# Two parts of the rows side by side in every other block of first products, experts of 208 and 192 slots

## The chip, the cores and the metric

The kernel runs on one core of a Trainium2 chip. TensorE (PE, with its weight loads as PEld) multiplies, VectorE (DVE) and ScalarE (ACT) read its sums out of PSUM, GpSimd (POOL) works on SBUF and issues indirect DMAs, SyncE (SP) issues most other DMAs. The metric is the device time of one execution in microseconds (us); lower is better.

## What is computed

A linear-attention recurrence, then two mixture-of-experts layers of 8 experts (1536 rows of 384, hidden width 1024). The change concerns the first of the layers alone:

```python
h = np.maximum(np.einsum('ecd,edf->ecf', disp, w1), 0.0)
y = np.einsum('ecf,efd->ecd', h, w2)
```

The first line is what is called "first products" here, the second "second products".

## The kernel before, in words

**Jobs.** The 16 experts (8 of layer 1, 8 of layer 2) are jobs 0 to 15, one after the other on TensorE. Jobs 0 and 1 have 240 slots; jobs 2 to 7 take the other six experts in order of their number of rows and have 240, 224, 208, 208, 192 and 192 slots (`CAPS`). So jobs 4 and 5 have 208 columns, 6 and 7 have 192. In the profiled execution job 4 starts at 159.5 us, job 5 at 176.7, job 6 at 194.4, job 7 at 211.0 and job 8 at 227.6.

**Split numbers.** TensorE multiplies fp32r numbers, which are rounded. To keep fp32 precision, each weight and each row is split into a high part (rounded, a copy by ScalarE, L537 for weights and L635 for rows) and a low part (the rest, a subtraction by GpSimd or VectorE, L538 and L636). A product is then high x high + low weight x high row + high weight x low row.

**First products (`hidden`).** A job has 8 blocks of 128 hidden columns, f = 0 to 7. A block is 9 matmuls into one PSUM bank: three parts of the depth (d), each with three products (six at L683, then the three with the low rows at L686). ScalarE then writes the rectified sum's high part (L692, "relu" below) and VectorE its low part (L693, "subtract"); both read the bank. There are three such banks (`ph`), used in turn: block f + 3 can start when VectorE's subtract of block f has ended.

**Second products (`second`).** For each f, three output parts: one matmul with the high weights over both halves of the hidden block side by side (2c columns, L714), one with the low weights over its high half (c columns, L716). In PSUM the two halves of the result stay apart; `job_route2` adds them when it reads them out (L841 on ScalarE, L842 on VectorE).

**What lies between.** Each engine takes its instructions strictly in the order in which the code issues them. Between the blocks of job n stand the steps of the routing of job n - 1 (`route2`, a generator, stepped by the table `STEPS`): 6 fp32 matmuls that show as 12 rows at L750 after block 1, two scaled copies on ScalarE (L752), then a chain of some thirty small VectorE instructions, a few ScalarE ones (L766, L767, L773, L800), three small matmuls that count places (L813 to L817, on TensorE's queue behind the second products of f = 0 to 2), and four indirect DMAs from GpSimd that scatter the rows for layer 2. The L813 matmul needs `accs`, written by VectorE at L796. Also between the blocks stand the splits of the next job's weights (L537, L538), one for each block.

In TensorE's order a layer-1 job is: blocks 0 and 1, L750, blocks 2 to 7, second products of f = 0 to 2, L813 to L817, second products of f = 3 to 7.

Of the kernel before, what the change touches and what calls it, by code (L numbers as in the profile page):

```python
# [7 lines left out]
F32R = mybir.dt.float32r  # L8
# [3 lines left out]
AF = mybir.ActivationFunctionType  # L12
ALU = mybir.AluOpType
# [8 lines left out]
C1, T1 = 240, 2  # L22
# [12 lines left out]
NF, ND = F // 128, DM // 128  # L35
# [19 lines left out]
LR = (5, 6, 7, 5, 7, 8)  # L55
LX = 9
SP = 7
WG = 8
STEPS = ("0111122111110000", "1232210200000000", "0100000111100000", "0111000000000000")
ENGS = ("GGGGGGGGGGGVVVVG", "GGGGGGGGGGGGGGGG")  # L60
# [7 lines left out]
def body(tc, ap, cap, dbg=False, stop=False):  # L68
    nc = tc.nc
    V, A, G, PE = nc.vector, nc.scalar, nc.gpsimd, nc.tensor  # L70
    with ExitStack() as ctx:
# [15 lines left out]
        def hb(shape, dt=F32):  # L87
            return sb(shape, "h", 18, dt)

        def xb(shape, dt=F32):  # L90
            return sb(shape, "x", 4, dt)
# [8 lines left out]
        def ph():  # L100
            return ps("ph", 3)
# [355 lines left out]
        jobs = [(1, e) for e in range(E)] + [(2, e) for e in range(E)]  # L457
# [87 lines left out]
        def w1_of(n, f, d):  # L545
            hi, lo = parts[n, f // 4]
            c = (f % 4) * 128
            return hi[:, d, c:c + 128], lo[:, d, c:c + 128]
# [6 lines left out]
        xg, xsp, xr_ = {}, {}, {}  # L555
# [34 lines left out]
        def load_rows(eng, g, rows_, c, cols):  # L590
# [5 lines left out]
                eng.dma_start(g[:c - k * p, k:, cols], rows_(k * p, c)[:, None, cols])  # L596
            eng.dma_start(g[:, :k, cols], rows_(0, k * p).rearrange("(t p) d -> p t d", p=p)[:, :, cols])

        def load_x(n, eng):
            layer, e = jobs[n]  # L600
            nt_, p, c = dims(n)
            store = (xs1, xs2)[layer - 1]
            if not turned(n):
                g = sb([p, nt_, RW], "b6", 5)
                load_rows(eng, g, lambda a, b: store[e * R + a:e * R + b], c, slice(None))
            else:
                nb = -(-c // 32)
                rows_of = lambda eng, r: store[e * R:e * R + r] if place(n) is None else store[bass.ds(expert(n, eng) * R, r), :]
                w = RW if layer == 1 else RW - DM
                t6 = sb([128, nb * ND * 32 + nt_ * w], "b6", 5)  # L610
                g = t6[:p, nb * ND * 32:].rearrange("p (t d) -> p t d", t=nt_)
                if layer == 2:
                    g = few_of(g)
                load_rows(eng, g, lambda a, b: rows_of(eng.engine, nt_ * p)[a:b], c if layer == 1 else nb * 32,
                          slice(DM, None))
                x = xr_[n] = t6[:, :nb * ND * 32].rearrange("p (t d) -> p t d", t=nb)
                rows_ = rows_of(mybir.EngineType.SP, nb * 32)
                for b in range(4):
                    nc.sync.dma_start(x[b * 32:b * 32 + 32], rows_.rearrange("(t j) d -> j t d", j=32)[
                        :, :, b * ND * 32:(b + 1) * ND * 32])  # L620
            xg[n] = g
            xsp[n] = (xb([128, ND, c], F32R), xb([128, ND, c], F32R))

        def split_x(n, d):
            layer, e = jobs[n]
            nt_, p, c = dims(n)
            g, (xh, xl) = xg[n], xsp[n]
            ds = (d,)
            if turned(n):
                x = xr_[n][:, :, d * 32:d * 32 + 32]  # L630
                y = pm()[:, :x.shape[1] * 32]
                V.transpose(y.rearrange("p (t j) -> p t j", j=32), x)  # L632

                def high():
                    A.activation(xh[:, d, :], y[:, :c], AF.Copy)  # L635
                    rest.append(lambda: V.tensor_tensor(xl[:, d, :], y[:, :c], xh[:, d, :].bitcast(F32), op=ALU.subtract))  # L636

                rest.append(high)
                return
            xp = pm()  # L640
            for k, d in enumerate(ds):
                for t, sl, r in tiles(n):
                    PE.transpose(xp[:, k * c + sl.start:k * c + sl.stop], g[:r, t, d * 128:(d + 1) * 128],
                                 ident[:r, :r])
            m = lambda x: x[:, ds[0]:ds[-1] + 1, :].rearrange("p d c -> p (d c)")
            w = len(ds) * c
            A.activation(m(xh), xp[:, :w], AF.Copy)
            V.tensor_tensor(m(xl), xp[:, :w], m(xh).bitcast(F32), op=ALU.subtract)

        def first_x():  # L650

            at = [py()[:, :C1] for _ in range(ND)]
            for d in range(ND):
                for t in range(T1):
                    PE.matmul(at[d][:, t * P1:(t + 1) * P1], early[0][:, t, d * 128:(d + 1) * 128], ident[:P1, :P1],
                              start=(t == 0), stop=False, skip_group_check=True)
            yield
            n = N // 128
            for j in range(EARLY, n):
                for d in range(ND):  # L660
                    for i in range(2):
                        PE.matmul(at[d], late[j][:, i * DM + d * 128:i * DM + (d + 1) * 128], late[j][:, 2 * DM:],
                                  start=False, stop=(i == 1 and j == n - 1), skip_group_check=True)
                yield
            xg[0] = sb([P1, T1, RW], "b6", 5)
            nc.sync.dma_start(xg[0][:, :, DM:], xs1[:C1, DM:].rearrange("(t p) d -> p t d", p=P1))
            xh, xl = xsp[0] = (xb([128, ND, C1], F32R), xb([128, ND, C1], F32R))
            for d in range(ND):
                A.activation(xh[:, d, :], at[d], AF.Copy)
                V.tensor_tensor(xl[:, d, :], at[d], xh[:, d, :].bitcast(F32), op=ALU.subtract)  # L670
            yield
# [2 lines left out]

        def hidden(n, f):
            c = dims(n)[2]
            xh, xl = xsp[n]
            p = ph()[:, :c]
            k = 0
            for d in range(ND):  # L680
                wh, wl = w1_of(n, f, d)
                for (w, x) in ((wh, xh), (wl, xh)):
                    PE.matmul(p, w, x[:, d, :], start=(k == 0), stop=False)  # L683
                    k += 1
            for d in range(ND):
                PE.matmul(p, w1_of(n, f, d)[0], xl[:, d, :], start=False, stop=(d == ND - 1))  # L686
            if jobs[n][0] == 1:
                both = hb([128, 2 * c], F32R)
                hh, hl = both[:, :c], both[:, c:]
            else:  # L690
                both, hh, hl = None, hb([128, c], F32R), hb([128, c], F32R)
            A.activation(hh, p, AF.Relu)  # L692
            V.scalar_tensor_tensor(hl, p, 0.0, hh.bitcast(F32), op0=ALU.max, op1=ALU.subtract)  # L693
            hs[f] = (hh, hl, both)
# [531 lines left out]
        for n, (layer, e) in enumerate(jobs):  # L1226
# [37 lines left out]
            if n < 2 * E - 1:  # L1264
                for f in range(NF):
# [14 lines left out]
                    if n == E and f == 0:  # L1280
                        for _ in prev:
                            pass
                        it, fin, d = late_tokens(n, gl), None, 0
# [31 lines left out]
            else:  # L1315
                nt_, p, c = dims(n)
# [229 lines left out]
```

## Time and profile before

| | |
|---|---|
| median of 3 runs | 457.77 us (457.44 to 458.2) |
| the profiled execution | 457.52 us |
| its span, first to last instruction | 455.8 us |
| outside the span | 1.7 us |
| TensorE busy | 444.1 us, 97% of the span |
| VectorE, ScalarE, GpSimd busy | 275.5, 265.6 and 345.9 us |

The profiled execution is 0.25 us below the median of the runs. Matmuls overlap, so their rows are longer than the distance from one start to the next; that distance is what a matmul costs on TensorE.

### The profile page before, as it was taken

Reading aid. Unit: us, or ns where it says so; the run is one execution under the profiler, and the core shown is the slowest. Engines: PE = TensorE matmul, PEld = TensorE weight load, DVE = VectorE, ACT = ScalarE, POOL = GpSimd, SP = SyncE. Lnnn points to the kernel's source line nnn. Section 1 sums busy time; section 2 is a strip of 40 time slices with the busy share of each in tenths; the row PEclk is TensorE's granted clock in tenths of the full one; section 3 lists DMA queues with packets and bytes.
Section 4 is the critical chain, followed back from the end, with each engine's and each line's share of the span. In section 5 each row is a group of like instructions: output and inputs, shape, how many; then the busy total and the mean of one; then the engine's idle time right before and its main releaser. Section 6 shows DMA issues by size and latency. Waiting matters only on the chain.

```text
span 455.8 us, 9510 instructions
## 1 busy us (share of the span) xinstructions
PE 444.1 (97%) x3167; PEld 417.8 (92%) x3170; DVE 275.5 (60%) x909; ACT 265.6 (58%) x703; POOL 345.9 (76%) x433
## 2 busy tenths in 40 slices
PE   8999999999999999999999999999999999999992
PEld 4588888899999999999999999999999999999992
DVE  8999988666967867878866454343434343243350
ACT  4577788367776775786651468255454464664310
POOL 4435698585998989899943379989969699699932
PEclk9999999999999999999999999999999999999998
DMA  8975962769999977976421997649378393894143
GB/s 279 408 265 160 350 239 97 246 206 317 332 294 317 276 257 220 261 228 195 127 70 55 267 318 220 137 111 295 75 227 188 91 313 75 253 282 54 18 53 43
DMA packets 73587, 93.66 MB, mean 205 GB/s; under 512 B 31963, under 2 KB 56611, under 8 KB 73527
## 3 DMA queue, kind: packets, MB, share of 16 engines
q1 hardware_dynamic: 66854, 79.98, 57.1%
q0 software_dynamic: 6672, 12.97, 12.7%
q8 instruction: 27, 0.44, 0.4%
q14 instruction: 34, 0.27, 0.2%
HBM read 70.30 MB, written 20.02 MB: 198 GB/s over the span
## 4 chain that ended last, share of the span: by engine, by line
PE 95%; DVE 2%; ACT 1%; issue 1%; POOL 0%; POOLq 0%; ACTq 0%
PE ph L683 24%; PE py L722 22%; PE ph L686 12%; PE py L714 9%; PE py L716 4%; PE ph L170 4%; PE ph L309 3%; PE pm L750 3%; PE pm L385 2%; PE py L336 2%; PE py L362 2%; PE py L356 2%; PE py L303 1%; PE ph L1002 1%; PE ph L975 1%; PE py L334 1%
## 5 line engine op out<-in xcount | busy, mean ns | idle before, releaser
L538 POOL TENSOR_TENSOR s<-s,s 128x384 fp32r<-128x384 f32 x208 | 217.7, 1173 | 17.9 <-ACT s L537 16.5
L683 PE MATMUL ph<-x,s 128*128 128x240 f32 (+9 forms) x768 | 133.0, 308 | 0.3 <-DVE h L693 0.3
L537 ACT ACTIVATE s<-s 128x384 fp32r<-128x384 f32 x256 | 124.7, 516 | 9.2 <-DMA s<-w 5.5
L683 PEld LDWEIGHTS ph<-x,s 128*128 128x128 f32 x768 | 116.2, 189 | 1.8 <-DVE h L693 0.5
L693 DVE SCALAR_TENSOR_TENSOR h<-ph,h 128x240 fp32r<-128x240 f32 (+9 forms) x128 | 60.2, 470 | 81.7 <-ACT h L692 76.4
L692 ACT ACTIVATE h<-ph 128x240 fp32r<-128x240 f32 (+9 forms) x128 | 54.1, 423 | 72.0 <-PE ph L686 68.4
L686 PE MATMUL ph<-x,s 128*128 128x240 f32 (+9 forms) x384 | 76.2, 306 | 0.0
L158 POOL DMA_INDIRECT out<-b,m_ix x28 | 44.0, 1571 | 30.2 <-ACT b L878 8.7
L722 PE MATMUL py<-h,s 128*128 128x304 f32 (+4 forms) x360 | 65.4, 339 | 0.0
L722 PEld LDWEIGHTS py<-h,s 128*128 128x128 f32 x360 | 63.2, 188 | 0.8
L714 PE MATMUL py<-h,s 128*128 128x480 f32 (+3 forms) x192 | 61.5, 376 | 0.0
L686 PEld LDWEIGHTS ph<-x,s 128*128 128x128 f32 x384 | 60.9, 189 | 0.2
L716 PE MATMUL py<-h,s 128*128 128x240 f32 (+3 forms) x192 | 50.5, 263 | 0.0
L158 POOL DMA_INDIRECT xs<-b,m_si x32 | 32.3, 1010 | 17.0 <-DVE pm L832 10.5
L318 POOL TENSOR_SCALAR_AFFINE_SELECT h<-h 128x512 f32<-128x512 f32 x24 | 23.8, 1014 | 27.9 <-ACT h L317 27.9
L722 PE MATMUL py<-s,h 128*128 128x384 f32 x216 | 38.6, 338 | 0.0
L714 PEld LDWEIGHTS py<-h,s 128*128 128x128 f32 x192 | 36.1, 188 | 2.6
L636 DVE TENSOR_TENSOR x<-pm,x 128x384 fp32r<-128x384 f32 (+8 forms) x42 | 19.9, 473 | 29.8 <-ACT x L635 29.6
L722 PEld LDWEIGHTS py<-s,h 128*128 128x128 f32 x216 | 37.8, 188 | 0.0
L716 PEld LDWEIGHTS py<-h,s 128*128 128x128 f32 x192 | 36.6, 191 | 0.0
L538 DVE TENSOR_TENSOR s<-s,s 128x384 fp32r<-128x384 f32 x48 | 34.0, 729 | 0.8 <-ACT s L537 0.5
L635 ACT ACTIVATE x<-pm 128x384 fp32r<-128x384 f32 (+8 forms) x42 | 17.7, 420 | 23.6 <-DVE pm L632 20.3
(263 smaller groups left out, 604.0 us busy)
## 6 DMA issues: line engine op xcount, KB each, us to landing
s<-w SPq DMA_DIRECT2D x28, 768.0 KB
s<-w_2b SPq DMA_DIRECT2D x22, 768.0 KB
s<-w_1b SPq DMA_DIRECT2D x14, 768.0 KB
xs<-s SPq DMA_DIRECT2D x2, 1576.0 KB
out<-s SPq DMA_DIRECT2D x4, 768.0 KB
b<-xs SPq DMA_DIRECT2D x12, 156.0 KB
b<-xs SPq DMA_DIRECT2D x12, 144.0 KB
b<-b SPq DMA_DIRECT2D x44, 36.0 KB
```

Of the source, the lines that this page charges most:

```text
L158: st = G.indirect_dma_start(out=dst, out_offset=bass.IndirectOffsetOnAxis(ap=ix, axis=0), in_=src, in_offset=None, **kw)
L318: G.affine_select(a_, a_, pattern=[[0, 4], [1, 128]], compare_op=ALU.is_ge, fill=0.0, base=0, channel_multiplier=-1)
L537: A.activation(hi[sl], t[sl], AF.Copy)
L538: rest.append(lambda: (eng or V).tensor_tensor(lo[sl], t[sl], hi[sl].bitcast(F32), op=ALU.subtract))
L636: rest.append(lambda: V.tensor_tensor(xl[:, d, :], y[:, :c], xh[:, d, :].bitcast(F32), op=ALU.subtract))
L683: PE.matmul(p, w, x[:, d, :], start=(k == 0), stop=False)
L686: PE.matmul(p, w1_of(n, f, d)[0], xl[:, d, :], start=False, stop=(d == ND - 1))
L692: A.activation(hh, p, AF.Relu)
L693: V.scalar_tensor_tensor(hl, p, 0.0, hh.bitcast(F32), op0=ALU.max, op1=ALU.subtract)
L714: PE.matmul(yp[o][:, :2 * c], wh[:, sl], both, start=(f == 0), stop=(f == NF - 1), skip_group_check=True)
L716: PE.matmul(yp[o][:, :c], wl[:, sl], hh, start=False, stop=(f == NF - 1), skip_group_check=True)
L722: PE.matmul(out_, l, r, start=(f == 0 and k == 0), stop=(f == NF - 1 and k == 2))
```

## The change

In jobs 4 to 7 the odd blocks (f = 1, 3, 5, 7) of the first products are built as the second products already are: for each d one matmul with the high weights over the high and the low rows side by side (2c columns, 416 or 384) and one with the low weights over the high rows (c columns). That is 6 matmuls in place of 9. The bank then holds two halves, c columns that are nearly the sum and c columns of high weight x low row. ScalarE copies the second half to SBUF, VectorE adds it to the first half in PSUM, and then relu and subtract follow as before. Even blocks and all other jobs stay as they are. For layer 1 the high and low rows of a job now lie in one tile.

```diff
+SIDE = 208
...
+        def two_parts(layer, c):
+            if layer == 2:
+                return xb([128, ND, c], F32R), xb([128, ND, c], F32R)
+            x = xb([128, ND, 2, c], F32R)
+            return x[:, :, 0, :], x[:, :, 1, :], x
...
-            xsp[n] = (xb([128, ND, c], F32R), xb([128, ND, c], F32R))
+            xsp[n] = two_parts(layer, c)
...
         def hidden(n, f):
             c = dims(n)[2]
-            xh, xl = xsp[n]
-            p = ph()[:, :c]
+            xh, xl = xsp[n][:2]
+            bank = ph()
+            p = bank[:, :c]
             k = 0
-            for d in range(ND):
-                wh, wl = w1_of(n, f, d)
-                for (w, x) in ((wh, xh), (wl, xh)):
-                    PE.matmul(p, w, x[:, d, :], start=(k == 0), stop=False)
-                    k += 1
-            for d in range(ND):
-                PE.matmul(p, w1_of(n, f, d)[0], xl[:, d, :], start=False, stop=(d == ND - 1))
+            if jobs[n][0] == 1 and c <= SIDE and f % 2:
+                for d in range(ND):
+                    wh, wl = w1_of(n, f, d)
+                    PE.matmul(bank[:, :2 * c], wh, xsp[n][2][:, d].rearrange("p k c -> p (k c)"), start=(d == 0),
+                              stop=(d == ND - 1), skip_group_check=True)
+                    PE.matmul(p, wl, xh[:, d, :], start=False, stop=(d == ND - 1), skip_group_check=True)
+                low = hb([128, c])
+                A.activation(low, bank[:, c:2 * c], AF.Copy)
+                V.tensor_tensor(p, p, low, op=ALU.add)
+            else:
...
```

How the instructions stand, at three places of job 4. First ScalarE from block 2's relu to block 4's. The tiles `ph_...` are the banks (480, 487, 489 are blocks 2, 3, 4 before; 475, 482, 485 after), `s6` weights, `m_u` a small tile of the routing. Before:

```order
L692 ACTIVATE h_481_2617<-ph_480_2607 128x208
L537 ACTIVATE s6_474_2577<-s6_461_2477 128x3x128
L692 ACTIVATE h_488_2642<-ph_487_2632 128x208
L766 ACTIVATE m_u_482_2622<-pm_478_2594 112x16
L767 ACTIVATE m_u_482_2622<-m_u_482_2622 112x16
L537 ACTIVATE s6_474_2577<-s6_461_2477 128x3x128
L692 ACTIVATE h_490_2659<-ph_489_2649 128x208
```

And in the changed kernel:

```order
L710 ACTIVATE h_476_2611<-ph_475_2601 128x208
L538 ACTIVATE s6_468_2571<-s6_456_2472 128x3x128
L695 ACTIVATE h_483_2633<-ph_482_2626 128x208
L710 ACTIVATE h_484_2636<-ph_482_2626 128x208
L784 ACTIVATE m_u_477_2616<-pm_473_2588 112x16
L785 ACTIVATE m_u_477_2616<-m_u_477_2616 112x16
L538 ACTIVATE s6_468_2571<-s6_456_2472 128x3x128
L710 ACTIVATE h_486_2653<-ph_485_2643 128x208
```

The copy (L695) stands directly ahead of block 3's relu (L710); nothing lies between the two that ScalarE could do while VectorE adds.

VectorE at the same place, from block 2's subtract to block 4's, before:

```order
L693 SCALAR_TENSOR_TENSOR h_481_2617<-ph_480_2607,h_481_2617 128x208
L755 TENSOR_TENSOR pm_478_2594<-pm_478_2594,b6_367_1961 112x32
L760 TENSOR_SCALAR pm_478_2594<-b6_367_1961 112x2
L761 SCALAR_TENSOR_TENSOR pm_478_2594<-pm_478_2594,io8_166 112x16
L763 TENSOR_TENSOR m_ti_485_2625<-tr2_178,pm_478_2594 112x4
L693 SCALAR_TENSOR_TENSOR h_488_2642<-ph_487_2632,h_488_2642 128x208
L693 SCALAR_TENSOR_TENSOR h_490_2659<-ph_489_2649,h_490_2659 128x208
```

And after:

```order
L711 SCALAR_TENSOR_TENSOR h_476_2611<-ph_475_2601,h_476_2611 128x208
L773 TENSOR_TENSOR pm_473_2588<-pm_473_2588,b6_364_1958 112x32
L778 TENSOR_SCALAR pm_473_2588<-b6_364_1958 112x2
L779 SCALAR_TENSOR_TENSOR pm_473_2588<-pm_473_2588,io8_166 112x16
L781 TENSOR_TENSOR m_ti_480_2619<-tr2_178,pm_473_2588 112x4
L696 TENSOR_TENSOR ph_482_2626<-ph_482_2626,h_483_2633 128x208
L711 SCALAR_TENSOR_TENSOR h_484_2636<-ph_482_2626,h_484_2636 128x208
L711 SCALAR_TENSOR_TENSOR h_486_2653<-ph_485_2643,h_486_2653 128x208
```

The add (L696) stands behind the routing's four small instructions and directly ahead of the subtract of its block.

VectorE at the end of the first products, from the routing's search for the two largest to the tile `accs`, before:

```order
L786 MAX m_m8_498_2705<-m_nl_497_2702 112x8 x2
L788 MAX_INDEX m_i8_499_2706<-m_m8_498_2705,m_nl_497_2702 112x8 x2
L693 SCALAR_TENSOR_TENSOR h_502_2724<-ph_501_2714,h_502_2724 128x208
L792 TENSOR_TENSOR m_oh2_503_2728<-pm_478_2594,m_i8_499_2706 112x16 x2
L796 TENSOR_REDUCE accs_190<-m_oh2_503_2728 112x16
```

And after:

```order
L804 MAX m_m8_495_2699<-m_nl_494_2696 112x8 x2
L806 MAX_INDEX m_i8_496_2700<-m_m8_495_2699,m_nl_494_2696 112x8 x2
L696 TENSOR_TENSOR ph_498_2708<-ph_498_2708,h_499_2715 128x208
L711 SCALAR_TENSOR_TENSOR h_500_2718<-ph_498_2708,h_500_2718 128x208
L810 TENSOR_TENSOR m_oh2_501_2722<-pm_473_2588,m_i8_496_2700 112x16 x2
L814 TENSOR_REDUCE accs_190<-m_oh2_501_2722 112x16
```

Block 7's add and subtract both stand ahead of the reduction that writes `accs`; before it was the subtract alone.

## Rows read from the trace of the kernel before

**Rows 1.** The page: busy time, share of the span, instructions of each engine.
```profile
PE 444.1 (97%) x3167; PEld 417.8 (92%) x3170; DVE 275.5 (60%) x909; ACT 265.6 (58%) x703; POOL 345.9 (76%) x433
```

**Rows 2.** Waits of TensorE, jobs 4 to 8: us in total, times, longest.
```profile
PE ph L683 <- DVE h L693: 0.3, 1, 0.3
```

**Rows 3.** Windows of jobs 4, 5: PE, PEld, DVE, ACT, POOL busy, clock, DMA.
```profile
159.50:176.70 17.20, 17.20 (x138) 17.03 (x136) 12.55 (x55) 11.88 (x37) 15.80 (x20) 1.00 0.82 255
176.70:194.40 17.70, 17.37 (x137) 17.02 (x136) 12.88 (x56) 12.30 (x38) 15.86 (x20) 1.00 0.82 240
```

**Rows 4.** Timeline of TensorE, job 4: start, length, what.
```profile
164.01 0.83 PE L683 MATMUL ph<-x,s 128*128 128x208 f32 x6
...
165.01 0.83 PE L683 MATMUL ph<-x,s 128*128 128x208 f32 x6
...
169.29 0.37 PE L714 MATMUL py<-h,s 128*128 128x416 f32 x1
...
169.59 0.36 PE L714 MATMUL py<-h,s 128*128 128x416 f32 x1
...
171.99 0.17 PE L813 MATMUL ph<-accs,tri 112*112 112x16 bf16 x1
```

**Rows 5.** Timeline of TensorE, job 6, the last pair ahead of L813.
```profile
206.19 0.36 PE L714 MATMUL py<-h,s 128*128 128x384 f32 x1
...
206.48 0.17 PE L813 MATMUL ph<-accs,tri 104*104 104x16 bf16 x1
```

**Rows 6.** Timeline of ScalarE, job 4: relu 1, 2, 3 and L766, [idle before <- releaser].
```profile
163.57 0.34 ACT L692 ACTIVATE h<-ph 128x208 fp32r<-128x208 f32 x1 [1.46 <-PE pm L750]
...
165.15 0.35 ACT L692 ACTIVATE h<-ph 128x208 fp32r<-128x208 f32 x1
...
165.79 0.36 ACT L692 ACTIVATE h<-ph 128x208 fp32r<-128x208 f32 x1
...
166.66 0.18 ACT L766 ACTIVATE m_u<-pm 112x16 f32<-112x16 f32 x1 [0.51 <-DVE m_ti L763]
```

**Rows 7.** Timeline of VectorE, job 4: subtracts 1, 2, 3 and 7, then L796.
```profile
163.95 0.38 DVE L693 SCALAR_TENSOR_TENSOR h<-ph,h 128x208 fp32r<-128x208 f32 x1 [1.84 <-ACT h L692]
...
165.54 0.38 DVE L693 SCALAR_TENSOR_TENSOR h<-ph,h 128x208 fp32r<-128x208 f32 x1 [0.43 <-ACT h L692]
...
166.54 0.36 DVE L693 SCALAR_TENSOR_TENSOR h<-ph,h 128x208 fp32r<-128x208 f32 x1
...
170.73 0.35 DVE L693 SCALAR_TENSOR_TENSOR h<-ph,h 128x208 fp32r<-128x208 f32 x1
...
171.28 0.19 DVE L796 TENSOR_REDUCE accs<-m_oh 112x16 bf16<-112x32 f32 x1
```

**Rows 8.** VectorE reading PSUM (three in a row), and writing PSUM.
```profile
178.05 0.94 DVE L842 TENSOR_TENSOR b<-py,b 128x208 f32<-128x208 f32 x3
...
171.46 0.43 DVE L632 STREAM_TRANSPOSE pm<-b 128x224 f32<-128x224 f32 x1
```

**Rows 9.** Job 5: ScalarE's relu 1, and TensorE's start of block 5.
```profile
181.32 0.35 ACT L692 ACTIVATE h<-ph 128x208 fp32r<-128x208 f32 x1 [2.19 <-PE ph L686]
...
183.71 0.92 PE L683 MATMUL ph<-x,s 128*128 128x208 f32 x6 [0.33 <-DVE h L693]
```

**Rows 10.** Job 6: ScalarE's relu 1, relu 2 and L766, VectorE's L796.
```profile
196.67 0.36 ACT L692 ACTIVATE h<-ph 128x192 fp32r<-128x192 f32 x1
...
199.31 0.33 ACT L692 ACTIVATE h<-ph 128x192 fp32r<-128x192 f32 x1 [0.20 <-PE ph L686]
...
200.77 0.18 ACT L766 ACTIVATE m_u<-pm 104x16 f32<-104x16 f32 x1 [0.34 <-DVE m_ti L763]
...
205.40 0.19 DVE L796 TENSOR_REDUCE accs<-m_oh 104x16 bf16<-104x32 f32 x1
```

**Rows 11.** A wait of TensorE in an earlier stage, and the window around it.
```profile
80.53 0.17 PE L429 MATMUL pm<-m_oh,ones 128*128 128x8 bf16 x1 [1.05 <-DVE m_oh L420]
...
80.00:88.00 8.00, 7.37 (x69) 6.63 (x68) 5.59 (x37) 2.85 (x9) 3.32 (x6) 1.00 0.93 311
```

More of the change, by code (lines that the diff above doesn't have):

```diff
@@ L626, in split_x @@
             nt_, p, c = dims(n)
-            g, (xh, xl) = xg[n], xsp[n]
+            g, (xh, xl) = xg[n], xsp[n][:2]
             ds = (d,)
@@ L666, in first_x @@
             nc.sync.dma_start(xg[0][:, :, DM:], xs1[:C1, DM:].rearrange("(t p) d -> p t d", p=P1))
-            xh, xl = xsp[0] = (xb([128, ND, C1], F32R), xb([128, ND, C1], F32R))
+            xh, xl, _ = xsp[0] = two_parts(1, C1)
             for d in range(ND):
@@ L676, in hidden @@
             c = dims(n)[2]
-            xh, xl = xsp[n]
-            p = ph()[:, :c]
+            xh, xl = xsp[n][:2]
+            bank = ph()
+            p = bank[:, :c]
             k = 0
-            for d in range(ND):
-                wh, wl = w1_of(n, f, d)
-                for (w, x) in ((wh, xh), (wl, xh)):
-                    PE.matmul(p, w, x[:, d, :], start=(k == 0), stop=False)
-                    k += 1
-            for d in range(ND):
-                PE.matmul(p, w1_of(n, f, d)[0], xl[:, d, :], start=False, stop=(d == ND - 1))
+            if jobs[n][0] == 1 and c <= SIDE and f % 2:
[8 more added lines that the diff above has]
+            else:
+                for d in range(ND):
+                    wh, wl = w1_of(n, f, d)
+                    for (w, x) in ((wh, xh), (wl, xh)):
+                        PE.matmul(p, w, x[:, d, :], start=(k == 0), stop=False)
+                        k += 1
+                for d in range(ND):
+                    PE.matmul(p, w1_of(n, f, d)[0], xl[:, d, :], start=False, stop=(d == ND - 1))
             if jobs[n][0] == 1:
```

## The prediction

> **What bounds the kernel now.** I read the page first. TensorE is busy for 97% of the span [rows 1], and in jobs 4 to 8 its only wait of size is one of 0.3 us, on VectorE's subtract [rows 2]. So what an expert costs TensorE goes straight into the time, and what makes TensorE wait does too. The other engines seem to have room: in the windows of jobs 4 and 5 VectorE works 12.6 to 12.9 us of 17.2 to 17.7, ScalarE 11.9 to 12.3 [rows 3]. That share is over the whole job, though. I therefore read the timelines of the first products, where the three PSUM banks go round. The reader should see there how tight the round is. Block f + 3 waits for subtract f. In job 4 blocks 3 to 7 take 169.29 - 164.01 = 5.28 us, 0.28 more than five times the 1.00 of one block [rows 4]: the banks already come back a little late. In job 5 that is worse by some 0.5 us (its window is 17.7 against 17.2 [rows 3]), and there TensorE waited 0.33 us for VectorE at block 5 [rows 9].
>
> **What the change takes away.** One wide and one narrow matmul cost 169.59 - 169.29 = 0.30 us from start to start at 208 columns [rows 4], and 0.29 at 192 [rows 5]. Three such pairs make 0.90 and 0.87 us in place of 1.00. These are the second products' own pairs, with the same weight loads, so I take them as they are. That is 0.10 us for each of 8 blocks and 0.13 for each of 8: 1.8 us less on TensorE if nothing waits.
>
> **What it adds.** Each odd block gets a ScalarE copy out of PSUM and a VectorE add. The copy has relu's shape: 0.34 us [rows 6]. No row shows an add of this width that reads and writes PSUM. Below, three L842 (which read PSUM and write SBUF) start 0.285 apart, since 0.94 = 0.37 + 2 x 0.285; above, a transpose of 224 columns that writes PSUM takes 0.43 [rows 8]. I take 0.38, nearest to the subtract of the same bank [rows 7]. Handing over costs 0.04: relu 1 ends at 163.91 and its subtract starts at 163.95 [rows 6, 7]. Copy, add, relu and subtract read or write the same columns and must follow each other, so the subtract of an odd block comes 0.34 + 0.38 + 2 x 0.04 = 0.80 us later than before. ScalarE stands still during the add, because relu is its next instruction. Behind it stand the next relu and the split of the next weights; behind the add stand the subtracts and the routing.
>
> **Job 4 step by step**, in the times of the trace before. ScalarE takes block 1 at 163.57, after 1.46 us without work [rows 6], and I assume that it does so again. Subtract 1 then starts at 163.95 + 0.80 = 164.75, ends at 165.13, and block 4 can start at 165.17. TensorE wants it at 164.01 - 0.10 + 0.90 = 164.81 [rows 4]: it waits 0.36. Relu 2 and subtract 2 come behind in order, also 0.80 later: subtract 2 runs from 166.34 to 166.72 [rows 7], block 5 starts at 166.76 and wanted 166.17: 0.59. Copy 3 runs from 166.59 [rows 6] to 166.93, but the add stands behind the routing's small instructions, which held subtract 3 until 166.54 before [rows 7] and now end 0.80 later, at 167.34. Add to 167.72, relu 167.76 to 168.10, subtract 168.14 to 168.50; block 6 starts at 168.54 and wanted 167.66: 0.88. Block 7's bank is back in time. The second products start at 168.54 + 1.00 + 0.90 = 170.44, where they started at 169.29: 1.15 us lost, the 0.4 us gain already counted.
>
> The larger item comes next. The matmul at L813 stands in TensorE's queue 171.99 - 169.29 = 2.70 us into the second products and needs the tile that VectorE writes at L796 [rows 4, 7]. It had 171.99 - 171.47 = 0.52 us to spare. Behind relu 3 ScalarE used to wait 0.51 us for the routing [rows 6]; that cushion goes, and L766 shifts from 166.66 to about 168.04, by 1.4. Blocks 5 and 7 add 0.80 each, because ScalarE has hardly a gap from there to block 7. Subtract 7 moves by 3.0, to 173.7; L796 follows 0.55 later [rows 7] and ends at 174.5. TensorE wants it at 170.44 + 2.70 = 173.14 and waits 1.4. Job 4 loses 1.15 + 1.4 = **2.5 us**.
>
> **Job 5** is the same with a worse start: relu 1 came at 181.32, 4.63 us into the job against 4.03 in job 4 [rows 6, 9], so block 4 waits 0.6 more. About as much of its waiting is in the time before. Again **2.5 us**.
>
> **Jobs 6 and 7.** Relu 1 came early in job 6, at 196.67, 2.24 us into it [rows 10]; the bank of block 1 is back long before block 4, and I expect next to no wait at blocks 4 to 6 (0 to 0.3). L813 stands at 206.48, L796 ended at 205.59 [rows 5, 10]: 0.89 to spare. Three late odd blocks shift L796 by 3 x 0.80 = 2.4, less the 0.54 that ScalarE waited for nothing else (0.20 and 0.34 [rows 10]): 1.86. TensorE arrives 0.4 earlier (its gain of 0.5, less 0.1 of waiting at block 6). So it waits 1.86 - 0.89 + 0.4 = 1.4, and gains 0.5: **0.9 us** lost, in each of the two.
>
> **What is handed on.** VectorE enters the second half of each job 0.5 us closer to TensorE than before (0.04 in place of 0.52 ahead of L813). It then still has to split the rows for the next job, at up to 0.5 us of wait; I take 0.1 in each of jobs 5 to 7, 0.3 in all.
>
> **The sum.** 2.5 + 2.5 + 0.9 + 0.9 + 0.3 = 7.1 us on the profiled execution's own 457.52, of which 455.8 is the span: 464.6. The median of the runs lies 0.25 above that execution, so **464.9 us**. Behind job 7 TensorE has no wait that the delay could fill [rows 2], so it is passed on whole. GpSimd, at 15.8 to 15.9 us of work in a job [rows 3], gets longer jobs, not shorter ones, and the new copies take buffers of a round of 18, of which a job of layer 1 now uses 12.
>
> **Bounds.** An add of 0.285 shortens each of the waits by 0.1: in jobs 4 and 5 three to four waits hang on it, in 6 and 7 the one at L813 with three adds ahead; some 1.5 us less in all. At 0.43 it is 0.8 more. The hand-over takes 0 to 1.5. The forecast's own range is 463 to 467.
>
> **Rivals.**
> - *Block 1 is taken up at once in jobs 4 and 5.* ScalarE was idle for 1.46 and 2.19 us there, waiting for TensorE [rows 6, 9], and the trace does not say why so long. If that does not happen again, blocks 4 and 5 do not wait, block 6 waits 0.3 and L813 1.3: 1.2 us a job after the gain of 0.4, less the 0.28 and 0.75 of waiting that before already held. 0.9 + 0.4 + 1.8 + 0.3 = 3.4: **461.2 us**. For it: jobs 6 and 7 have it so. Against: both jobs that matter showed it.
> - *Faster.* ScalarE and VectorE have 4 to 5 us free in a job [rows 3], and four copies and four adds come to 1.4 and 1.5. If they fit, TensorE's 1.8 us is the result: **456.0 us**. It decides where an odd block adds less than the slack at each meeting point: under about 0.2 us, against L813's 0.52 with three or four odd blocks ahead of it. The 0.80 speaks against it; it would need copies and adds that overlap relu and subtract.
> - *No difference.* The gain of 1.8 and two or three waits at L813 alone of 0.6 us cancel: **457.8**, if ScalarE's other waits swallow half of each odd block's 0.80.
> - *The clock falls.* In the trace before, a wait of 1.05 us left the granted clock at 1.00, the 2.4 GHz level, in its window [rows 11]. Waits of 0.4 to 1.4 us now come four to a job. At the level of 1.2 GHz a matmul takes up to twice as long, so 3 us of work done at it would cost up to 3 us more: **468 us**. The Trainium skill ("TensorE: Matmul & The Clock Gate", section "A second HAM failure mode: psum-queue depth-cycling") tells of a kernel in which short idle spells between groups of matmuls, from going round the PSUM banks, made the clock swing between its levels and cost throughput. The row above does not bear that out for one wait alone; no run here shows four in a row.
>
> **Chances.** Forecast 0.72; block 1 at once 0.12; faster 0.06; no difference 0.04; clock or a longer cascade through GpSimd 0.06. The range 461 to 467.5 takes in the second case and the bounds of the first. A measurement of this kernel tells 0.2%, 0.9 us, from no change: faster 0.06, the same 0.04, slower 0.90.
>
> **What would show it.** Right: TensorE's waits name VectorE's subtract at the start of blocks 4, 5 and 6 of jobs 4 and 5 (0.4, 0.6 and 0.9 us), and VectorE's L814 (the old L796) at L831 (the old L813) in all four jobs, by about 1.4. Right on the gain: an odd block's six matmuls start 0.90 and 0.87 us before the next block where that doesn't wait. Wrong: L831 without a wait, an add well off 0.38, relu 1 of jobs 4 and 5 close behind its block, or a job 8 that starts less than 5 us later than at 227.6.

## The result, and the profile after

The changed kernel takes **463.01 us** (median of 7 runs, 462.52 to 463.91), the kernel before 457.77 beside it. The ratio is 1.0111, with a 95% interval of 1.0091 to 1.0130: 5.2 us slower. In a second comparison it was 463.35 against 457.72, 1.0126 (1.0109 to 1.0142). The profiled execution took 463.91 us, with a span of 462.2.

In the lines of the kernel after, the odd blocks' matmuls are L691 (wide) and L693 (narrow), the even blocks' L701 and L704, the copy L695, the add L696, relu L710, the subtract L711. L796 has become L814, and L813 has become L831.

The page's line of busy time answers to [rows 1]:

```profile
PE 444.8 (96%) x3119; PEld 416.0 (90%) x3122; DVE 277.2 (60%) x925; ACT 268.7 (58%) x719; POOL 344.6 (75%) x433
```

VectorE's and ScalarE's busy time goes up by only 1.7 and 3.1 us, less than the 5.9 and 5.4 us that the 16 adds and 16 copies take by themselves (0.37 and 0.34 each): on ScalarE rows overlap, which busy time counts once, and VectorE's 48 splits of weights take 3.5 us less. TensorE has 48 matmuls fewer. Nothing in this line says that 5 us were lost. TensorE's waits in jobs 4 to 8, the view of [rows 2], do:

```profile
PE ph L831 <- DVE accs L814: 2.9, 3, 1.0
PE ph L701 <- DVE h L711: 1.4, 3, 0.6
PE ph L831 <- ACT m_ge L818: 1.0, 1, 1.0
PE ph L691 <- DVE h L711: 0.7, 2, 0.3
```

One wait of 0.3 us has become nine of 6.0 us together: four at L831, one in each job, and five for subtracts. (The fourth at L831 is put down to a ScalarE instruction that stands next to L814; it is the same stop.) TensorE in job 4, where [rows 4] has no gap:

```profile
165.51 0.26 PE L693 MATMUL ph<-x,s 128*128 128x208 f32 x1
165.95 0.92 PE L701 MATMUL ph<-x,s 128*128 128x208 f32 x6 [0.17 <-DVE h L711]
166.71 0.49 PE L704 MATMUL ph<-x,s 128*128 128x208 f32 x3
167.54 0.46 PE L691 MATMUL ph<-x,s 128*128 128x416 f32 x1 [0.33 <-DVE h L711]
...
168.43 0.26 PE L693 MATMUL ph<-x,s 128*128 128x208 f32 x1
169.32 0.92 PE L701 MATMUL ph<-x,s 128*128 128x208 f32 x6 [0.63 <-DVE h L711]
...
173.93 0.26 PE L734 MATMUL py<-h,s 128*128 128x208 f32 x1
175.15 0.22 PE L831 MATMUL ph<-accs,tri 112*112 112x16 bf16 x1 [0.96 <-DVE accs L814]
```

The idle time in brackets is counted from a matmul's end, which overlaps the next one; what is lost is read from start to start. A narrow matmul normally gives way after 0.10 us, so block 4 was wanted at 165.61 and came at 165.95 (0.34 lost), block 6 at 168.53 and came at 169.32 (0.79), L831 at 174.03 and came at 175.15 (1.12). Block 5, after three L704 at 0.11 each, was wanted at 167.04 and lost 0.50.

Where the time comes from is seen on ScalarE, again in job 4:

```profile
164.35 0.34 ACT L695 ACTIVATE h<-ph 128x208 f32<-128x208 f32 x1 [1.45 <-PE pm L768]
165.14 0.34 ACT L710 ACTIVATE h<-ph 128x208 fp32r<-128x208 f32 x1 [0.45 <-DVE ph L696]
...
167.36 0.36 ACT L695 ACTIVATE h<-ph 128x208 f32<-128x208 f32 x1
168.52 0.34 ACT L710 ACTIVATE h<-ph 128x208 fp32r<-128x208 f32 x1 [0.80 <-DVE ph L696]
...
172.27 0.35 ACT L695 ACTIVATE h<-ph 128x208 f32<-128x208 f32 x1
173.96 0.34 ACT L710 ACTIVATE h<-ph 128x208 fp32r<-128x208 f32 x1 [1.33 <-DVE ph L696]
```

Behind each copy ScalarE stands still until VectorE has added. In block 7 that is 1.33 us, because the add itself stands behind the routing's small instructions:

```profile
173.07 0.24 DVE L804 MAX8 m_m<-m_nl 112x8 f32<-112x8 f32 x2
...
173.56 0.36 DVE L696 TENSOR_TENSOR ph<-ph,h 128x208 f32<-128x208 f32 x1
174.33 0.38 DVE L711 SCALAR_TENSOR_TENSOR h<-ph,h 128x208 fp32r<-128x208 f32 x1 [0.41 <-ACT h L710]
174.62 0.25 DVE L810 TENSOR_TENSOR m_oh<-pm,m_i 112x16 f32<-112x16 f32 x2
174.91 0.19 DVE L814 TENSOR_REDUCE accs<-m_oh 112x16 bf16<-112x32 f32 x1
```

Over jobs 4 to 7 this idle time of ScalarE, which the kernel before doesn't have, is the largest of all its waits:

```profile
ACT h L710 <- DVE ph L696: 10.9, 14, 1.3
```

The lengths of the jobs, from the first matmul of one to the first of the next (job 7: to the first block of job 8), say what each job lost. They are worked out from the starts in the timelines, and all experiments are in the table already:

| us | job 4 | job 5 | job 6 | job 7 |
|---|---|---|---|---|
| before, the trace of the prediction | 17.15 | 17.74 | 16.53 | 19.07 |
| before, once more (c1_before) | 17.19 | 17.69 | 16.52 | 19.81 |
| after | 19.55 | 19.26 | 17.69 | 19.36 |
| after, once more (c2_after) | 19.54 | 18.87 | 17.71 | 19.34 |
| e1_accs_first | 17.70 | 19.25 | 18.20 | 20.11 |
| e2_nine | 18.70 | 19.24 | 17.70 | 19.55 |
| e3_no_sum | 16.56 | 17.45 | 16.12 | 19.61 |
| e4_relu_late | 17.87 | 18.29 | 16.69 | 18.58 |
| e10_late_ahead_of_split | 18.04 | 18.57 | 17.18 | 19.40 |
| in the group at 455.46 us: e5_only_192 | 16.89 | 16.93 | 17.28 | 19.32 |
| e6_copy_only | 16.52 | 16.50 | 15.95 | 19.42 |
| e8_late_192 | 16.89 | 16.92 | 16.65 | 18.40 |
| e9_add_only | 17.67 | 17.80 | 17.36 | 19.18 |

After against before: 2.40, 1.52, 1.16 and 0.29, together 5.4 us. The changed kernel's trace is also 0.8 us late before job 4 begins (160.34 against 159.54); the second one is not (159.52), so that is no part of the change.

### The profile page after: what moved, and what is told of

Read it like the earlier page. It is cut to its first block, busy times and chain, and to the rows that moved or that the text cites. A ratio compares the mean times of both kernels' runs of the same rounds, so it can differ in the third digit from the quotient of the medians.

```text
span 462.2 us, 9447 instructions
## 1 busy us (share of the span) xinstructions
PE 444.8 (96%) x3119; PEld 416.0 (90%) x3122; DVE 277.2 (60%) x925; ACT 268.7 (58%) x719; POOL 344.6 (75%) x433
## 4 chain that ended last, share of the span: by engine, by line
PE 85%; DVE 7%; ACT 4%; issue 1%; POOL 0%; POOLq 0%; ACTq 0%; DVEq 0%
PE py L740 22%; PE ph L701 20%; PE ph L704 10%; PE py L732 7%; PE ph L171 4%; PE py L734 3%; PE ph L310 3%; PE pm L768 2%; PE pm L386 2%; PE py L337 2%; PE py L363 2%; PE py L357 2%; ACT h L710 1%; ACT s L538 1%; PE py L304 1%
## 5 line engine op out<-in xcount | busy, mean ns | idle before, releaser
L701 PE MATMUL ph<-x,s 128*128 128x240 f32 (+9 forms) x672 | 119.7, 313 | 1.6 <-DVE h L711 1.4
L711 DVE SCALAR_TENSOR_TENSOR h<-ph,h 128x240 fp32r<-128x240 f32 (+9 forms) x128 | 60.2, 471 | 82.7 <-ACT h L710 79.7
L701 PEld LDWEIGHTS ph<-x,s 128*128 128x128 f32 x672 | 104.0, 189 | 3.6 <-DVE h L711 2.8
L710 ACT ACTIVATE h<-ph 128x240 fp32r<-128x240 f32 (+9 forms) x128 | 53.9, 422 | 85.0 <-PE ph L704 71.5
L704 PE MATMUL ph<-x,s 128*128 128x240 f32 (+9 forms) x336 | 68.2, 311 | 0.0
L704 PEld LDWEIGHTS ph<-x,s 128*128 128x128 f32 x336 | 54.4, 189 | 0.2
L319 POOL TENSOR_SCALAR_AFFINE_SELECT h<-h 128x512 f32<-128x512 f32 x24 | 22.8, 971 | 30.2 <-ACT h L318 30.2
L159 POOL DMA_INDIRECT xs<-b,m_si x32 | 32.3, 1009 | 17.3 <-DVE pm L850 10.9
L539 DVE TENSOR_TENSOR s<-s,s 128x384 fp32r<-128x384 f32 x48 | 30.5, 657 | 0.8 <-ACT s L538 0.5
L642 ACT ACTIVATE x<-pm 128x384 fp32r<-128x384 f32 (+8 forms) x42 | 17.7, 420 | 19.9 <-DVE pm L639 18.0
```

The lines of the kernel that those rows point to most:

```text
L159: st = G.indirect_dma_start(out=dst, out_offset=bass.IndirectOffsetOnAxis(ap=ix, axis=0), in_=src, in_offset=None, **kw)
L319: G.affine_select(a_, a_, pattern=[[0, 4], [1, 128]], compare_op=ALU.is_ge, fill=0.0, base=0, channel_multiplier=-1)
L539: rest.append(lambda: (eng or V).tensor_tensor(lo[sl], t[sl], hi[sl].bitcast(F32), op=ALU.subtract))
```

## The experiments

Kernels that ran together form a group, and each is compared with the kernel before in its own group. The first four runs had 457.69 us for it, the next four (e5, e6, e9, e8) 455.46, the last four 457.72. The record numbers the chip of the first group 2 and that of both other groups 15, so the chip's number does not explain the 2.3 us.

**1. Is the wait at L831 only the queue order on VectorE?** The routing's step with L810 and L814 is issued ahead of block 7's add and subtract.

```diff
-STEPS = ("0111122111110000", ...
+STEPS = ("0111123011110000", ...
```

> The changed kernel, with one number moved in the list of steps: the routing's two steps that read the accumulator (the pair at L810 and L814, for whose end TensorE waits 1.14 us at L831 four times, jobs 4 to 7) are issued ahead of the add and the subtract of block 7 instead of behind them. Theory one, the wait at L831 is only the queue order on VectorE: it goes in all four jobs, 4 x 1.14 = 4.5 us come back, time about 458.8 (458 to 460). Theory two, VectorE's and ScalarE's whole chain of a job is late and only pays at the next stop: block 7's subtract moves later, TensorE waits for it at the second products (L732 or L734) or at a block of the next job, and less than 2 us come back, time 461 to 463.

462.86 us, ratio 1.0116 (1.0094 to 1.0138): nothing is won, theory two. The waits at L831 are gone, and TensorE's largest waits in jobs 4 to 7 now read:

```profile
PE ph L701 <- ACT x L642: 2.7, 3, 1.0
PE ph L701 <- DVE h L711: 1.3, 2, 0.6
```

Job 4 is 1.85 us shorter than after, jobs 6 and 7 are longer by 0.5 and 0.75. The wait has moved to the first block of the next job, which needs the rows that ScalarE splits at L642. That copy waits 1.45 us for VectorE's transpose, which stands behind VectorE's late work:

```profile
178.97 0.34 ACT L642 ACTIVATE x<-pm 128x208 fp32r<-128x208 f32 x1 [1.45 <-DVE pm L639]
```

So L831 is only the first place at which TensorE meets a chain that is late as a whole.

**2. What is TensorE's gain worth beside that chain?** The odd blocks take nine matmuls again, with copy and add kept.

```diff
-    PE.matmul(bank[:, :2 * c], wh, xsp[n][2][:, d].rearrange("p k c -> p (k c)"), ...
-    PE.matmul(p, wl, xh[:, d, :], ...
+    for w in (wh, wl):
+        PE.matmul(p, w, xh[:, d, :], ...
...
+for d in range(ND):
+    PE.matmul(bank[:, c:2 * c], w1_of(n, f, d)[0], xl[:, d, :], ...
```

> The changed kernel, but the odd blocks take nine matmuls again (the three of the rows' low part go to the second half of the bank); the copy on ScalarE and the add on VectorE stay. TensorE thus gets nothing, and all that follows the block is as late as in the changed kernel. Theory one, TensorE's 0.10 to 0.13 us for each of 16 odd blocks is lost at the next wait, since the chain of copy, relu, add and subtract sets the pace: time that of the changed kernel, 463.0 (462.3 to 463.8). Theory two, what TensorE saves counts in full beside the chain: 463.0 + 1.8 = 464.8 (464.2 to 465.5).

462.40 us, 1.0109 (1.0086 to 1.0132): theory one. With all of the gain taken away the kernel is not slower. Jobs 5 to 7 are as long as after, within 0.2 us. (Job 4 is 0.85 shorter: there the copy of block 1 came 0.99 us after its last matmul and not 1.95.)

**3. The gain alone.** Copy and add are left out.

```diff
-                low = hb([128, c])
-                A.activation(low, bank[:, c:2 * c], AF.Copy)
-                V.tensor_tensor(p, p, low, op=ALU.add)
```

> The changed kernel without the copy on ScalarE and the add on VectorE in the odd blocks: the second half of the bank is left unread, so the high weight times the low part of the rows is missing from the odd blocks. What stays of the change is the wide matmul and the other layout of the two parts. Theory one, the whole loss is the two added instructions, and the wide matmul gives 0.10 to 0.13 us for each of 16 odd blocks: 457.8 - 1.8 = 456.0 (455.3 to 456.8). Theory two, the layout of the parts side by side or the wide matmul itself costs something too (a slower split, a slower read of the rows): 457.5 or more.

457.08 us, 0.9987 (0.9975 to 0.9999): between the two theories. Jobs 4 to 6 took 50.13 us, against 51.42 before, 1.29 less for a calculated 8 x 0.10 + 4 x 0.13 = 1.3. That the sum meets so well is partly luck: job by job it is 0.59, 0.29 and 0.41 for 0.40, 0.40 and 0.52, probably because ScalarE's late starts (experiments 10 to 12) differ between the two traces. Cleaner are jobs 4 and 5 of two runs without such starts: e6_copy_only has six matmuls in the odd blocks there, e5_only_192 nine, and the jobs are 0.37 and 0.43 us shorter for 0.40. In job 7 TensorE now waits at its first block and at its end:

```profile
210.75 0.47 PE L698 MATMUL ph<-x,s 128*128 128x192 f32 x2 [0.50 <-issue]
...
227.76 0.33 PE L650 MATMUL pm<-iw,b 128*128 128x128 f32 x1 [0.36 <-DVE x L655]
```

Whether this is where gain is lost is not shown: job 7's 19.61 us lies between the two traces of before, 19.07 and 19.81. But even a sum that cost nothing would have made the kernel faster by only 0.6 us. The layout of the parts costs nothing that can be seen: all jobs of layer 1 have it, and job 3, which has nothing else of the change, lasts 17.31 us in both traces of before and both of after.

**4. Is it the durations or the order of issue?** Copy and add stay; relu and subtract of an odd block are issued at the end of its round.

```diff
+            def finish():
+                A.activation(hh, p, AF.Relu)
+                V.scalar_tensor_tensor(hl, p, 0.0, hh.bitcast(F32), op0=ALU.max, op1=ALU.subtract)
+            if jobs[n][0] == 1 and c <= SIDE and f % 2:
+                return finish
+            finish()
...
                     split(n + 1, f, eng[f])
+                    if end is not None:
+                        end()
```

> The changed kernel with the odd blocks' relu and subtract issued at the end of the block's round, behind the split and the routing steps, instead of directly behind the add; copy and add stay where they are. In the changed kernel ScalarE stands idle before the odd block's relu, while VectorE adds, for 0.45 to 1.33 us. Theory one, it is the order of issue on ScalarE and VectorE that makes the chain late: the other work of the round fills that idle time, the waits at blocks 5 and 6 shrink, and 1.5 to 3 us come back, time 460 to 461.5. Theory two, the two engines have no room left in these jobs, whatever the order: the odd block's subtract comes later still, its second product waits at L732 or L734, time 463 or more.

458.93 us, 1.0027 (1.0016 to 1.0038): better than theory one asked. With the same instructions, 4.1 us of the 5.3 come back. ScalarE's wait for the add over jobs 4 to 7, against 10.9 us above:

```profile
ACT h L713 <- DVE ph L696: 2.1, 4, 0.5
```

What is left is TensorE waiting for the odd blocks' subtracts, which are now late because they were issued late:

```profile
PE ph L701 <- DVE h L714: 2.9, 6, 0.9
```

**5. Half of the change.** `SIDE = 192`: only jobs 6 and 7.

> The changed kernel with the limit SIDE at 192: only the odd blocks of jobs 6 and 7 (192 slots) take both parts side by side, jobs 4 and 5 (208 slots) are as before. In the changed kernel jobs 6 and 7 were 1.16 and 0.29 us longer than before. Theory one, each job pays for its own odd blocks: 457.7 + 1.45 = 459.2 (458.6 to 459.8). Theory two, a good part of what jobs 6 and 7 lose was handed to them by the late end of ScalarE's and VectorE's work in job 5: under 458.3.

456.75 us against 455.46, 1.0029 (1.0018 to 1.0040): +1.3, theory one. Each job pays for its own odd blocks; jobs 6 and 7 would lose this without jobs 4 and 5.

**6 and 7. Copy without add, add without copy.**

```diff
                 A.activation(low, bank[:, c:2 * c], AF.Copy)
-                V.tensor_tensor(p, p, low, op=ALU.add)
```

> The changed kernel with ScalarE's copy but without VectorE's add (the copy's result is not used, so the high weight times the low part of the rows is missing from the odd blocks). Between the run without both (457.08) and the changed kernel (463.0) lie 5.9 us. Theory one, what counts is how much later the odd block's subtract ends: 0.34 us for the copy of 0.80 for both, so 457.1 + 0.43 x 5.9 = 459.6 (458.8 to 460.5). Theory two, only VectorE is short of time and the copy is hidden in ScalarE's idle time: 457.1 to 457.7. Theory three, ScalarE's extra read is what costs: over 461.

455.27 us, 0.9994 (0.9984 to 1.0004): theory two. The copy costs 0.4 us over the run without both (-0.2 against -0.6 us, each beside its own kernel before), which the two intervals do not tell from nothing.

```diff
-                low = hb([128, c])
-                A.activation(low, bank[:, c:2 * c], AF.Copy)
-                V.tensor_tensor(p, p, low, op=ALU.add)
+                V.tensor_tensor(p, p, xh[:, 0, :].bitcast(F32), op=ALU.add)
```

> The changed kernel with VectorE's add but without ScalarE's copy (the add takes a row tile that is there already instead of the copied half, so the odd blocks' values are not the reference's). Theory one, what counts is how much later the odd block's subtract ends: 0.42 us for the add of 0.80 for both, so 457.1 + 0.52 x 5.9 = 460.2 (459.3 to 461). Theory two, VectorE's time and the relu that waits for it are the whole price: 462 to 463. Theory three, the add is hidden: under 457.7.

458.69 us, 1.0065 (1.0052 to 1.0078): +3.2, so 3.8 over the run without both: at the upper end of theory one (457.7 + 3.2 = 460.9). But theory one is refuted by the pair: the lengths of copy and add are nearly the same, 0.34 and 0.38 us, and one costs 0.4, the other 3.8 (in one group, 455.27 against 458.69 us). What differs is that relu follows a copy on its own engine but must wait for an add on the other. That VectorE's added work alone is the price does not fit: e4_relu_late has the same adds and loses 1.2 us, not 5.3. ScalarE's waits, and TensorE's, in jobs 4 to 7 of the run with the add:

```profile
ACT h L708 <- DVE ph L694: 14.5, 16, 1.6
...
PE ph L829 <- DVE accs L812: 3.4, 4, 0.9
```

(L829 is the same stop as L831.) Copy and add together cost 5.9 us over the run without them, 1.7 more than one by one. One reading is that the copy is hidden as long as ScalarE has slack, and that the add's wait takes the slack. It is not shown: the comparison crosses groups with and without ScalarE's late starts (experiments 10 to 12).

**8. The best order, in the two jobs where it lost least.** Experiment 4 with `SIDE = 192`.

> The kernel with the odd blocks' relu and subtract at the end of the round (as in the run e4_relu_late, 458.93), and only in jobs 6 and 7 (limit 192). In e4_relu_late jobs 4 to 7 were 0.72, 0.55 and 0.17 us longer and 0.49 us shorter than before. Theory one, each job's figure stands for itself: 457.7 + 0.17 - 0.49 = 457.4 (457.0 to 457.7), the best version so far that computes the reference. Theory two, job 7 was shorter only because job 8's start is set by something that does not move with the job's start, and given back late arrival: 457.7 to 458.3.

455.30 us, 0.9996 (0.9988 to 1.0005): inside the range of theory one (0.9985 to 1.0000 as a ratio), and no difference that can be told. It is the best version of the change, and no gain.

**9. An earlier place for relu.** Experiment 4 with the two lines at `split` exchanged.

> As the run e4_relu_late (1.0027 of before), but the odd blocks' relu and subtract are issued ahead of the split of the next job's weights instead of behind it: one step earlier, 0.52 us of ScalarE's time. In e4_relu_late TensorE still waits six times, 2.9 us in all, at L701 for the odd block's subtract, now too late. Theory one, the routing's steps alone fill the time of the add, the subtract comes 0.5 us earlier, and these waits go: ratio 0.998 to 1.000. Theory two, in the rounds that have no routing work for ScalarE (from block 12 on, and where a step waits for VectorE itself) the idle time before the relu is back: ratio 1.003 to 1.008.

460.65 us, 1.0063 (1.0050 to 1.0077): theory two. Without ScalarE's weight split in between, its wait for the add is half back:

```profile
ACT h L713 <- DVE ph L696: 5.4, 8, 1.2
```

**10 to 12. Why is block 1 taken up late, and does the kernel matter?** Both kernels once more, and the changed one with the scatters' step moved from block 11 to block 15.

> The kernel before, unchanged, profiled beside the three that follow. In the profile that the prediction rests on, ScalarE's relu of block 1 came 1.87 us (job 4) and 2.45 us (job 5) after the block's last matmul; in the runs e5_only_192 and e8_late_192 the same blocks of jobs 4 and 5, whose code is nearly that of before, were taken up after 0.04 us. Theory one, the lateness belongs to the execution or the chip and not to the kernel: it can be absent here, and jobs 4 and 5 then last about 16.9 us each and not 17.15 and 17.75. Theory two, it belongs to the kernel before, and the other layout of the parts removed it: it is here again, 1.5 us or more in job 5.

The one execution took 458.88 us; only its rows are used. Relu 1 of jobs 4 and 5, to be read against [rows 6, 9]:

```profile
163.61 0.34 ACT L692 ACTIVATE h<-ph 128x208 fp32r<-128x208 f32 x1 [1.42 <-PE pm L750]
...
180.00 0.35 ACT L692 ACTIVATE h<-ph 128x208 fp32r<-128x208 f32 x1 [0.82 <-PE pm L750]
```

It is late again in job 4 (1.91 us after the block's last matmul), and less late in job 5 (1.09 for 2.45). In e5_only_192, in the group at 455.46 us, the same blocks with nine matmuls:

```profile
161.30 0.34 ACT L710 ACTIVATE h<-ph 128x208 fp32r<-128x208 f32 x1 [0.25 <-PE ph L704]
...
178.21 0.34 ACT L710 ACTIVATE h<-ph 128x208 fp32r<-128x208 f32 x1 [0.25 <-PE ph L704]
```

Both came after 0.04 us. So the lateness differs between executions of one kernel. The layout of the parts does not decide it: in c2_after, which has the layout, it is there in job 4 (1.93 us), and e5_only_192 has the layout too. It goes with the group: in each of the ten traces with a kernel before of 457.7 us ScalarE stands idle, four to eight times in jobs 2 to 7, before taking up a block whose matmuls have ended, always while the scatters run or within 1.2 us behind them; in the four traces of the group at 455.46 us it takes such a block up within 0.04 us every time.

The times at which the trace notes semaphores going up (the counts by which engines wait for each other) narrow it down. The late relu 1 of job 4 before waits for TensorE's count alone. The block's last matmul ended at 161.71, but after 161.33 that count goes up only at 163.55, and then five times up to 163.75, for matmuls that ended between 161.71 and 163.18. In e5_only_192 the same step comes 0.01 us after the matmul's end (161.28 for 161.27). So what is late is the count that tells of the matmuls; TensorE itself went on to its next matmuls without a pause.

> The changed kernel, unchanged, profiled beside the kernel before. First comparison: +5.2 us, jobs 4 to 7 longer by 2.40, 1.52, 1.16 and 0.29 us, where job 5 of before had a late block 1 and job 5 of the changed kernel had not. Theory one, without late blocks on either side the four jobs lose more evenly, job 5 as much as job 4: +5 to +6 us in all, job 5 +2 or more. Theory two, job 5 loses only 1.5 us for a reason of its own: job 5 +1.5 again.

463.35 us, 1.0126. Job 5 lost 1.18 us (18.87 against 17.69), so theory two in the number; but theory one's condition, no late blocks on either side, was not met: block 1 of job 5 was late before (1.09 us) and hardly after (0.48).

```diff
-STEPS = ("0111122111110000", ...
+STEPS = ("0111122111100001", ...
```

> The changed kernel with the routing's last step, which issues the four scatters on GpSimd, moved from block 11 to block 15 of each job, so that the scatters run later, further into the next job. Theory one, the late taking up of block 1 follows the scatters (its copy came 0.82 us after the last scatter's end in job 4): it goes from block 1 or moves to a later block. Theory two, it has nothing to do with them: where the changed kernel beside it shows a late block 1, this one does too, and the time stays within 0.5 us of it.

478.24 us, 1.0446 (1.0429 to 1.0463): theory two missed, and theory one is borne out where it can be read, in job 2, which has no odd block in two parts. Blocks 1 and 3 there:

```profile
126.92 0.37 ACT L710 ACTIVATE h<-ph 128x240 fp32r<-128x240 f32 x1 [0.22 <-issue]
...
131.59 0.37 ACT L710 ACTIVATE h<-ph 128x240 fp32r<-128x240 f32 x1 [0.76 <-PE ph L704]
```

Block 1 is taken up 0.04 us after its last matmul, block 3 after 1.20, 1.01 behind the end of the last scatter (130.58). In c2_after, in the same group, it is 1.11 for block 1, 0.83 behind the last scatter, and 0.04 for block 3. The lateness has moved with the scatters; job 3 shows the same at block 3 (1.27 against 0.11). Neither theory foresaw the time. A wait that the changed kernel doesn't have, for the rows of the routing, now leads TensorE's list in jobs 4 to 7:

```profile
PE pm L768 <- DVE b L860: 4.7, 4, 1.4
```

How the scatters' place leads to it was not followed, and the run says nothing on what the lateness costs.

## Why the prediction was right, and where its terms were off

Sign and mechanism came as forecast. The time, 463.01 us, is 1.9 under the forecast's 464.9 and only just inside its range (463 to 467); that it lies inside owes something to luck, since job 5, job 7 and the hand-over were all sized too high. Step by step:

- **The gain on TensorE** was right: pairs start 0.30 us apart, and e6_copy_only against e5_only_192 shows 0.37 and 0.43 us a job for 0.40. That it is lost beside the waits is shown by e2_nine.
- **The add** at 0.38 us was right (0.36 to 0.38 in job 4).
- **Job 4** was right: waits of 0.34, 0.50 and 0.79 us at blocks 4 to 6 for the 0.36, 0.59 and 0.88 worked out. The second products were forecast at 170.44 - 159.54 = 10.90 us into the job, and could start at 169.32 + 1.00 + 0.90 - 160.34 = 10.88. L831 waited 1.12 for 1.4, since L814 ended 14.76 us into the job and not 14.96. The job lost 2.40 for 2.5.
- **Job 5** is the term that was most off: 1.52 and 1.18 us for 2.5. The step that failed is "the same with a worse start". It took relu 1's late start, 4.63 us into the job, as belonging to the kernel. In the changed kernel the copy stood at 182.46, 2.57 into the job, and block 4 did not wait. The job before had itself lost 0.8 us by the lateness: it lasts 16.93 us in e5_only_192, where the block is taken up at once. Matmul by matmul, counted from the job's start, the two agree within 0.01 us up to block 3; before is 0.63 us behind in block 5 and 0.85 at the end of block 7. Against that length the changed job 5 (19.26 and 18.87) loses 1.9 to 2.3 us. So the time before already held a part of the loss. How much of the rest is the change's own stays open, because the changed job was not free of late counts either: in the first trace they hit the scaled copies behind block 1, whose last matmul had ended at 183.58.

```profile
184.64 1.05 ACT L770 ACTIVATE b<-pm,b 104x384 f32<-104x384 f32 x2 [1.05 <-PE ph L704]
```

  The first rival, block 1 taken up at once, came nearly true in job 5 (0.50 and 0.48 us, behind other work of ScalarE) and not in job 4.
- **Jobs 6 and 7** were forecast at 0.9 each and came to 1.16 and 0.29, the second time 1.19 and -0.47. The waits at L831 were 1.15 and 1.14 for 1.4, and block 6 of job 6 waited 0.28 instead of 0.1. Job 7 ends at job 8's first block, behind matmuls that also wait for VectorE (0.7 us in the second trace of before); that the two kernels meet there part of the way is the likely reason, not a shown one.
- **Handed on**, 0.3 us, was wrong: TensorE's waits after show none at the start of a job. It becomes true when L831's stop is taken away (e1_accs_first).
- **Behind job 7** the delay is passed on whole, as said: job 8's first block is 6.17 us later in the trace, job 15's 6.47, of which 0.8 had come before job 4.
- **The rivals.** Faster was wrong as a forecast, and its condition, copies and adds that fit between the others, is nearly met by another order (e4_relu_late); but TensorE's 1.8 us were not to be had either. The clock did not fall, and GpSimd was not drawn in. Windows of jobs 4 to 7, columns as in [rows 3]:

```profile
160.30:179.90 19.60, 17.50 (x126) 16.51 (x124) 13.55 (x59) 12.74 (x41) 15.67 (x19) 1.00 0.78 231
179.90:199.10 19.20, 17.26 (x125) 16.41 (x124) 14.03 (x60) 13.40 (x42) 15.90 (x21) 1.00 0.72 216
199.10:216.80 17.70, 16.59 (x125) 16.02 (x124) 13.62 (x60) 12.92 (x41) 16.23 (x21) 1.00 0.65 213
216.80:234.40 17.60, 16.57 (x124) 15.55 (x123) 13.81 (x59) 13.62 (x43) 16.49 (x22) 1.00 0.39 124
```

The granted clock is 1.00, the 2.4 GHz level, in all four. The Trainium skill ("TensorE: Matmul & The Clock Gate", section "A second HAM failure mode: psum-queue depth-cycling") describes a clock that swings when the engine goes round its PSUM banks with short idle spells. Here one to four idle spells of 0.3 to 1.1 us in a job, counted from start to start as above, did not do that.

What the prediction did not see is how much of the price lies in the order of issue alone. It reckoned the subtract 0.80 us later for each odd block and took the order as given; e4_relu_late has the same durations and loses a quarter as much.

## What to carry to other kernels

Two short instructions that hand a tile from one in-order engine to another and back can cost a good part of their length, even on engines that look idle: here 11.3 us of copies and adds cost 5.9 us, though VectorE and ScalarE are busy for only 60 and 58% of the span. The first engine stands still until the other has got round to it, and everything behind it is late. Look for work to issue between the two, and price such a chain at the next place where a third engine meets it. If taking that wait away only moves it to the next meeting point (as here from L831 to the next job's first block), the chain is late, not the place. And before counting on time saved on the busiest engine, ask what it will wait for when it arrives earlier: here a free sum would have given 0.6 us of 1.8.

## What the runs showed of the hardware

- An add that reads one operand from PSUM and writes there (128 x 208, fp32) took 0.36 to 0.38 us on VectorE, as long as the subtract that reads the same bank and writes SBUF (0.36 to 0.38).
- ScalarE's start on block 1 of job 5 came 2.45 us after the block's last matmul in one execution of the kernel before, 1.09 in another, and 0.04 in the nearly equal code of e5_only_192. In e2_nine, e3_no_sum and e4_relu_late it began within 0.03 us of the end of the last of GpSimd's four scatters in job 4 (162.96 and 162.95, 162.55 and 162.58, 162.95 and 162.94); in both traces of before 0.8 us after it (163.57 and 162.79, 163.61 and 162.85); in e5_only_192 before it (161.30 and 161.90). What is late is TensorE's count, by up to 2.4 us, and it is late only while the scatters run or just behind them: with the scatters issued later (e7_scatters_late) the lateness moves from block 1 to block 3. What holds the count up stays open, and so does why it does not happen in the group at 455.46 us, where the scatters run as well (in e5_only_192 from 156.95 to 161.90). Such a stall is worth up to 0.8 us a job here, and should not be counted on to come again.
- The kernel before took 455.46 us in one group of runs and 457.7 in the others, one of which the record gives the same chip number, 15. The group at 455.46 us is the one whose traces show no late counts; that these are the 2.3 us is not shown.
